# Coarser routing groups, rows stored from ScalarE's queue, a shared ring of banks, and two jobs moved from VectorE to ScalarE

## The chip, the cores and the metric

The kernel runs on one core of one Trainium2 chip. The metric is the device time of one execution in microseconds (us), taken as the median of several runs. The engines are named as in the profile: PE is TensorE, DVE is VectorE, ACT is ScalarE, POOL is GpSimd, SP is SyncE.

## The reference

A gated linear attention over 4 batches, 8 heads, 768 steps and 48 features feeds two mixture-of-experts layers of 3072 tokens, 384 features, 8 experts and 1024 hidden features. In the first layer a token takes part only if its skip score is positive; each token goes to one expert.

```python
# attention, for every step t of a batch and head
state = alpha[:, :, t, :, None] * state + np.einsum('bhd,bhe->bhde', k[:, :, t], v[:, :, t])
y[:, :, t] = np.einsum('bhd,bhde->bhe', q[:, :, t], state)
# first layer (x: tokens by the 384 features of all heads)
do_compute = x @ w_skip > 0
e_idx = np.argmax(xc @ w_gate, axis=1)      # xc: the rows that compute
y[mask] = gate_w[mask, None] * (np.maximum(xc[mask] @ w1[e], 0.0) @ w2[e])   # for each expert e
out[do_compute] = xc + y
# second layer: the same without the skip and without adding x
```

## The kernel before

The attention is cut into 24 chunks of 128 steps (4 batches of 6). The loop over `g` (L744) issues, for each chunk, `emit_a(g + 1)`, `prep(g + 3)`, `emit_y(g)` and `emit_r(g - 1)`, so that four chunks are in work at once. Every engine runs its own instructions in the order in which they are issued.

`prep` runs two scans on DVE (L546 `pp`, L550 `qka`) and two multiplications on POOL (L554, L555). `emit_a` computes the scores `ap` of both halves on PE (L566), masks half 0 on DVE (L574) and half 1 on ACT and POOL (L571, L572), and transposes the keys into `kp` (L581), which ACT copies out (L583); the last chunk of a batch has no `kp`. `emit_y` starts the new state `sp` from the old one (L599; not in the first chunk of a batch), multiplies scores by values into `yp` (L605, L606), adds keys by values to `sp` (L610, L611) and state by queries to `yp` (L614, L615). ACT then copies `yp` out (L618) and DVE multiplies `sp` by the decay, giving the state `s` of the next chunk (L621); the last chunk of a batch has no `sp`. `emit_r` turns the chunk into rows of tokens and router logits at once (`rp`, L642); ACT copies the rows (L643) into a tile `xr` and DVE adds up the logits (L644).

PSUM tiles come from `bank(tag, ...)`: tag B is a ring of four banks (`ap` 0, `ap` 1, `sp`, `yp`), tag K is a single bank, shared by `kp` and `rp`. A tile's first writer waits for the last reader of the tile that held the bank before it.

`route(i)` picks the expert of the tokens of group `i` and works out their places in the experts' lists. It is a generator of small DVE steps; `rt()` runs some of them at points between the attention's instructions (about ten a chunk), so they lie in DVE's queue between the scans. There are 8 groups of 3 chunks (`GROUPS`); `SPLIT` is the number of groups whose tokens (18 chunks) expert list 0 takes. When a group is done, SP's queue stores its rows to `xrows` in DRAM (L679): 384 features, then gate, token number and 8 logits, `ROW` = 394 numbers each. POOL gathers the rows of an expert from there (L441). Small operands (`spot`, `kept`) lie in one PSUM bank of their own.

After chunk 23 the two layers follow, 9 blocks each; their instructions are not touched, except that they take their small operands from the same `spot` places and the same `index`. At `g == 0` two constant matrices are converted (`upper`, `ones`, L757 and L758) and small constants are copied (L761).

Of the kernel before, what the change touches and what calls it, by code (L numbers as in the profile page):

```python
# [8 lines left out]
F32 = mybir.dt.float32  # L9
# [3 lines left out]
AF = mybir.ActivationFunctionType  # L13
ALU = mybir.AluOpType
AX = mybir.AxisListType
# [5 lines left out]
C = 128  # L21
# [22 lines left out]
FIRST = 65536.0  # L44
SX = 64.0
GSCALE = 1.0 / SX
GROUPS = [3] * 8
SPLIT = 6
NWARM = 13

RT = [1, 1, 1, 1, 1, 1, 1, 1, 1, 1, 1, 1, 1, 1, 1, 1, 0, 2, 0, 2, 10, 10, 7, 14]
# [57 lines left out]
def body(tc, qka, vN, rw, wg2, wg17, w1a, w2a, w1b, w2b, cst, zr, out):  # L109
# [3 lines left out]
    with ctx:  # L113
# [6 lines left out]
        def cc(name):  # L120
            o, w = CST[name]
            return cs[:, o:o + w]
# [12 lines left out]
        with ExitStack() as fctx, tc.manual_schedule():  # L135
# [124 lines left out]

            def softmax_pick(l, n, w, res, scale=1.0):

                mx = spot("mx", 6, n, w)
                V.tensor_reduce(mx, l, axis=AX.X, op=ALU.max)
                yield 0
                sh = sm.tile([128, n, w, 8], F32, tag=f"sh{w}", name="sh")
                V.tensor_tensor(sh, l, mx.rearrange("p a (b o) -> p a b o", o=1).to_broadcast([128, n, w, 8]), op=ALU.subtract)
                ex = sm.tile([128, n, w, 8], F32, tag=f"ex{w}", name="ex")
                A.activation(out=ex, in_=sh, func=AF.Exp, scale=scale)
                yield 0  # L270
                eq = sm.tile([128, n, w, 8], F32, tag=f"eq{w}", name="eq")
                de = kept["desc"].rearrange("p (a e) -> p a e", a=1).to_broadcast([128, n * w, 8])
                V.scalar_tensor_tensor(out=eq.rearrange("p a b e -> p (a b) e"), in0=sh.rearrange("p a b e -> p (a b) e"),
                                       scalar=0.0, in1=de, op0=ALU.is_ge, op1=ALU.mult)
                yield 0
                V.tensor_reduce(mx, eq, axis=AX.X, op=ALU.max)
                yield 0
                V.tensor_tensor(eq, eq, mx.rearrange("p a (b o) -> p a b o", o=1).to_broadcast([128, n, w, 8]), op=ALU.is_equal)
                res += [eq, ex]
                yield 0  # L280

            def gates(ex, n, w, res):
                den = spot("den", 6, n, w)
                V.tensor_reduce(den, ex, axis=AX.X, op=ALU.add)
                yield 0
                V.tensor_scalar(den, den, 1e-9, None, op0=ALU.add)
                yield 0
                gw = sm.tile([128, n, w], F32, tag="gw", name="gw") if w == 2 else den
                V.reciprocal(gw, den)
                res.append(gw)  # L290
                yield 0
# [47 lines left out]
            def index(i, n, nl, ohm, on, rk, cols, region, first, last):  # L339

                ad = sm.tile([128, n, nl], F32, tag=f"ad{nl}", name="ad")
                V.tensor_tensor(ad, rk, ohm, op=ALU.mult)
                held[0] = False
                yield 0
                r = sm.tile([128, n, 1], F32, tag=f"r{nl}", name="r")
                V.tensor_reduce(r[:, :, 0], ad, axis=AX.X, op=ALU.add)
                yield 0
                ge = sm.tile([128, n, 4], F32, tag=f"ge{nl}", name="ge")
                V.tensor_tensor(ge, r.to_broadcast([128, n, 4]), kept["th"].rearrange("p (o e) -> p o e", o=1).to_broadcast([128, n, 4]), op=ALU.is_ge)
                yield 0  # L350

                tl = spot("tl", 3, n, 1)
                V.tensor_reduce(tl[:, :, 0], ge, axis=AX.X, op=ALU.add)
                yield 0
                ti = spot("ti", 24, n, 2, 4)
                V.tensor_tensor(ti, cc("seq")[:, 0:4].rearrange("p (a o e) -> p a o e", a=1, o=1).to_broadcast([128, n, 2, 4]),
                                tl.rearrange("p a (o e) -> p a o e", o=1).to_broadcast([128, n, 2, 4]), op=ALU.is_equal)
                yield 0
                pm = sm.tile([128, n, 1], F32, tag=f"pm{nl}", name="pm")
                V.scalar_tensor_tensor(out=pm, in0=tl, scalar=-128.0, in1=r, op0=ALU.mult, op1=ALU.add)  # L360
                w = 8 * sum(t for _, t in cols)
                mv = sm.tile([128, n, 2, w], F16, tag=f"mv{nl}", name="mv")
                o = 0
                for j0, t in cols:
                    V.tensor_tensor(
                        mv.rearrange("p a h c -> p (a h) c")[:, :, o:o + 8 * t].rearrange("p a (e t) -> p a e t", t=t),
                        on.rearrange("p a h e -> p (a h) e")[:, :, j0:j0 + 8].rearrange("p a (e o) -> p a e o", o=1).to_broadcast([128, 2 * n, 8, t]),
                        ti.rearrange("p a h t -> p (a h) t")[:, :, 0:t].rearrange("p a (o t) -> p a o t", o=1).to_broadcast([128, 2 * n, 8, t]), op=ALU.mult)
                    o += 8 * t
                yield 0  # L370
                hot = sm.tile([128, n, 128], F16, tag=f"hot{nl}", name="hot")
                V.tensor_tensor(hot, kept["iota"].rearrange("p (o c) -> p o c", o=1).to_broadcast([128, n, 128]), pm.to_broadcast([128, n, 128]), op=ALU.is_equal)
                yield 1
                yield from wait("indexed", i)
                done["indexed"] += 1
                for k in range(n):
                    T.matmul(idx_ps[:, region, :, NCOL - w:], lhsT=hot[:, k, :], rhs=mv[:, k], start=(first and k == 0), stop=(last and k == n - 1))
                if last:
                    yield 0
                    yield 0  # L380
# [205 lines left out]
            def emit_y(g):  # L586
# [31 lines left out]
                    A.activation(out=y[:, p0:p0 + n], in_=yp, func=AF.Copy)  # L618
                if step_s:
                    sn = wk.tile([GP, NP, D], F32, tag="s", name="s")  # L620
                    V.tensor_tensor(sn, sp, pt.pop(g)[:, :, C:C + 1].to_broadcast([GP, NP, D]), op=ALU.mult)  # L621
                    st["s", g + 1] = sn
                    rt(2)
                if n < NP:
# [9 lines left out]
            def emit_r(g):  # L634

                i, k, n, _ = gof[g]
                if k == 0:
                    xr[i] = em.tile([128, n, ROW], F32, tag="xr", name="xr", bufs=3)
                y = st.pop(("ys", g))
                rp = bank("B" if g == NB - 1 else "K", "rp", NP, 113)  # L640
                for p in range(NP):
                    T.matmul(rp[:, p, :], lhsT=y[:, p, :], rhs=rws[:, p, :], start=True, stop=True)  # L642
                A.activation(out=xr[i][:, k, 0:DM].rearrange("p (a b) -> p a b", a=NP), in_=rp[:, :, 0:96], func=AF.Copy)  # L643
                V.tensor_reduce(lg[:, g, :], rp[:, :, 96:113].rearrange("p a b -> p b a"), axis=AX.X, op=ALU.add)  # L644
                release()
                rt(3)

            def route(i):
# [2 lines left out]
                x = xr[i]  # L651
                l = lg[:, g0:g0 + n, :]
                res = []
                cm = spot("cm", 6, n, 2, 1)
                V.tensor_scalar(cm[:, :, 0, :], l[:, :, 0:1], 0.0, None, op0=ALU.is_gt)
                V.tensor_scalar(cm[:, :, 1, :], l[:, :, 0:1], 0.0, None, op0=ALU.is_le)
                yield from softmax_pick(l[:, :, 1:17].rearrange("p a (w e) -> p a w e", w=2), n, 2, res)
# [6 lines left out]
                def row_ends():  # L664
                    yield from count(n, ohm, before, cum[:, i + 1, :])
                    if i == SPLIT - 1:
                        V.tensor_copy(cum1, cum[:, SPLIT, :])
                        V.memset(cum1[:, 0:1], 0.0)
                    done["counted"] += 1
                    res = []  # L670
                    yield from gates(ex, n, 2, res)
                    den = res[0]
                    V.tensor_tensor(den, den, cm[:, :, :, 0], op=ALU.mult)
                    yield 0
                    V.tensor_reduce(x[:, :, GATE], den, axis=AX.X, op=ALU.add)
                    V.tensor_copy(x[:, :, TOK], kept["tok"][:, g0:g0 + n])
                    V.tensor_tensor(x[:, :, LOG:], l[:, :, 9:17], kept["one"].rearrange("p (a o) -> p a o", o=1).to_broadcast([128, n, 8]), op=ALU.mult)
                    yield 0
                    SY.dma_start(xrows[1 + g0 * 128:1 + (g0 + n) * 128, :].rearrange("(k p) d -> p k d", p=128), x)  # L679

                side = [start(row_ends())]
                on = numbered(n, 16, ohm, g0) if i == len(GROUPS) - 1 else None
# [61 lines left out]
            for g in range(NB):  # L744
# [9 lines left out]
                        finish(*routes[max(i - 2, 0):max(i - 1, 0)])  # L754
                        routes.append(start(route(i)))
                if g == 0:
                    V.tensor_copy(upper, cc("upper"))  # L757
                    V.tensor_copy(ones, cc("ones"))  # L758
                    for name, w in (("desc", 8), ("tok", NB), ("iota", 128), ("seq", 8)):
                        kept[name] = spot(name, w, w, bufs=1)  # L760
                        V.tensor_copy(kept[name], cc(name))  # L761
                    nb = NB + len(TILES1)
# [463 lines left out]
```

## Time and profile before

| what | value |
| --- | --- |
| time, median of 3 runs | 537.44 us (537.41 to 537.68) |
| time of the profiled execution | 539.43 us |
| its span in the profile | 537.7 us |
| mean granted clock of PE | 0.981 |
| busy shares of the span | PE 92%, DVE 69%, ACT 48%, POOL 49% |

The span runs from the first to the last instruction of the profiled execution; some 1.7 us lie around it. A busy share is an average over the attention (until about 154 us) and the two layers behind it.

### The profile page before, as it was taken

What the parts mean: (1) busy time and instruction counts of PE and PEld (TensorE: products, weight loads), DVE (VectorE), ACT (ScalarE), POOL (GpSimd) and SP (SyncE); (2) the same over time, 40 slices, a digit from 0 to 9 for tenths busy, and PEclk for the clock granted to TensorE, in tenths of its full rate; (3) what the DMA queues carried; (4) which work ended last, traced back from release to release, by engine and by line L of the source; (5) the groups of instructions that cost most, each with busy time, mean ns of one, the idle gap of its engine ahead of it and who ended that gap; (6) DMA issues with size and microseconds to landing.
All of it is one profiled execution on the core that took longest, in us unless ns stands there. A gap on an engine that the chain in (4) does not pass through costs nothing.

```text
span 537.7 us, 12030 instructions
## 1 busy us (share of the span) xinstructions
PE 496.3 (92%) x4704; PEld 381.6 (71%) x4704; DVE 371.5 (69%) x1031; ACT 256.4 (48%) x466; POOL 262.3 (49%) x226
## 2 busy tenths in 40 slices
PE   5889898998988999999879989999999999999993
PEld 3678787877877899989879757465555566666662
DVE  7978999999876868888768846863636364646320
ACT  1324343444433566566556415653546364646420
POOL 2366958668625666876947341416215150402121
PEclk9989999999999999999989999999999999999997
DMA  8756877425246667676874158473444535360010
GB/s 304 258 190 209 314 250 264 159 114 208 82 173 209 198 249 229 218 260 199 301 245 145 41 196 275 149 244 123 165 147 140 176 118 208 103 223 28 16 39 26
DMA packets 41460, 96.74 MB, mean 180 GB/s; under 512 B 3641, under 2 KB 28471, under 8 KB 41398
## 3 DMA queue, kind: packets, MB, share of 16 engines
q1 hardware_dynamic: 36662, 82.40, 45.0%
q0 software_dynamic: 4736, 13.51, 7.3%
q8 instruction: 39, 0.64, 0.5%
q14 instruction: 23, 0.19, 0.1%
HBM read 83.41 MB, written 12.99 MB: 179 GB/s over the span
## 4 chain that ended last, share of the span: by engine, by line
PE 56%; DVE 28%; DMA 5%; issue 5%; POOL 2%; ACT 2%; POOLq 0%; DVEq 0%; ACTq 0%
PE hp L464 8%; PE hp L463 8%; PE hp L465 8%; DVE pp L546 6%; DVE qka L550 5%; PE ypc L487 4%; PE ypc L488 4%; PE ypc L489 4%; DMA raw<-in_w1a 3%; PE yp L489 3%; PE yp L488 3%; PE yp L487 3%; PE tp L450 3%; POOL w0l L207 2%; DVE at L574 1%
## 5 line engine op out<-in xcount | busy, mean ns | idle before, releaser
L978 POOL DMA_INDIRECT out<-o,ixo x31 | 31.3, 1009 | 142.2 <-ACT o L1051 125.2
L469 DVE SCALAR_TENSOR_TENSOR h2l<-hp,h2h 128x352 f16<-128x352 f32 (+8 forms) x66 | 38.6, 585 | 64.0 <-ACT h2h L468 63.2
L465 PE MATMUL hp<-x2h,w0l 128*128 128x352 f16 (+8 forms) x216 | 68.7, 323 | 0.0
L463 PE MATMUL hp<-x2h,w0h 128*128 128x352 f16 (+8 forms) x216 | 68.7, 323 | 0.0
L464 PE MATMUL hp<-x2l,w0h 128*128 128x352 f16 (+8 forms) x216 | 68.7, 323 | 0.0
L207 POOL TENSOR_TENSOR w1l<-raw,w1h 128x768 bf16<-128x768 f32 (+1 forms) x26 | 43.0, 1681 | 28.2 <-ACT w1h L202 13.7
L463 PE MATMUL hp<-xh,w0h 128*128 128x200 f16 (+7 forms) x216 | 54.0, 257 | 2.5 <-DVE hl L469 1.4
L468 ACT ACTIVATE h2h<-hp 128x352 f16<-128x352 f32 (+8 forms) x66 | 33.8, 513 | 46.9 <-PE hp L465 45.2
L202 ACT ACTIVATE w0h<-raw 128x768 f16<-128x768 f32 x64 | 53.4, 836 | 4.6 <-DMA raw<-in_w1a 2.7
L441 POOL DMA_INDIRECT xg<-xrows,ix x41 | 49.1, 1197 | 11.6 <-issue 9.8
L464 PEld LDWEIGHTS <-w0h 128*128 128x128 f16 x432 | 43.0, 100 | 16.3 <-issue 3.0
L464 PE MATMUL hp<-xl,w0h 128*128 128x200 f16 (+7 forms) x216 | 53.9, 257 | 0.5 <-DVE xl L452 0.3
L465 PEld LDWEIGHTS <-w0l 128*128 128x128 bf16 x432 | 43.0, 100 | 15.6 <-issue 0.7
L465 PE MATMUL hp<-xh,w0l 128*128 128x200 f16 (+7 forms) x216 | 53.9, 257 | 0.0
L488 PE MATMUL yp<-hl,w1h 128*128 128x200 f16 (+7 forms) x216 | 53.4, 255 | 0.5 <-DVE hl L469 0.5
L487 PE MATMUL yp<-hh,w1h 128*128 128x200 f16 (+7 forms) x216 | 53.5, 255 | 0.0
L202 ACT ACTIVATE w1h<-raw 128x768 f16<-128x768 f32 x64 | 51.5, 836 | 4.1 <-DMA raw<-in_w2a 3.8
L489 PE MATMUL yp<-hh,w1l 128*128 128x200 f16 (+7 forms) x216 | 53.4, 255 | 0.0
L463 PEld LDWEIGHTS <-w0h 128*128 128x128 f16 x432 | 43.0, 100 | 13.6 <-issue 0.5
L554 POOL TENSOR_TENSOR qka<-qka 128x512 f32<-128x512 f32 (+1 forms) x24 | 27.5, 1147 | 47.1 <-DVE qka L550 35.7
L207 DVE TENSOR_TENSOR w0l<-raw,w0h 128x768 bf16<-128x768 f32 x38 | 39.7, 1044 | 14.4 <-ACT w0h L202 12.2
L207 POOL TENSOR_TENSOR w0l<-raw,w0h 128x768 bf16<-128x768 f32 (+1 forms) x26 | 43.2, 1685 | 5.0 <-ACT w0h L202 3.8
(183 smaller groups left out, 1346.2 us busy)
## 6 DMA issues: line engine op xcount, KB each, us to landing
qka<-in_qka SPq DMA_DIRECT2D x21, 772.0 KB, 6.0
raw<-in_w1a SPq DMA_DIRECT2D x8, 1536.0 KB, 6.6
raw<-in_w2a SPq DMA_DIRECT2D x8, 1536.0 KB, 9.4
raw<-in_w1b SPq DMA_DIRECT2D x8, 1536.0 KB, 7.9
raw<-in_w2b SPq DMA_DIRECT2D x8, 1536.0 KB, 7.0
xrows<-xr SPq DMA_DIRECT2D x8, 591.0 KB, 3.7
v<-in_vN SPq DMA_DIRECT2D x24, 192.0 KB, 5.1
xrows<-x SPq DMA_DIRECT2D x9, 197.0 KB, 4.1
```

Of the source, the lines that this page charges most:

```text
L202: A.activation(out=hi[:, sl], in_=r[:, sl], func=AF.Copy)
L207: eng.tensor_tensor(lo[:, sl], r[:, sl], hi[:, sl], op=ALU.subtract)
L441: P.indirect_dma_start(out=dst, out_offset=None, in_=xrows[0:rows], in_offset=bass.IndirectOffsetOnAxis(ap=ix, axis=0), bounds_check=rows ...
L463: T.matmul(hp[:, i], lhsT=wh[:, k, f], rhs=xh[:, k, 0:n], start=(k == 0), stop=False)
L464: T.matmul(hp[:, i], lhsT=wh[:, k, f], rhs=xl[:, k, 0:n], start=False, stop=False)
L465: T.matmul(hp[:, i], lhsT=wl[:, k, f], rhs=xh[:, k, 0:n], start=False, stop=(k == 2))
L468: A.activation(out=hh[:, f0:f0 + nf, 0:n], in_=hp, func=AF.Relu)
L469: V.scalar_tensor_tensor(out=hl[:, f0:f0 + nf, 0:n], in0=hp, scalar=0.0, in1=hh[:, f0:f0 + nf, 0:n], op0=ALU.max, op1=ALU.subtract)
L487: T.matmul(yp, lhsT=wh[:, f, ds], rhs=hs[0][:, f, c0:c1], start=(f == 0), stop=False)
L488: T.matmul(yp, lhsT=wh[:, f, ds], rhs=hs[1][:, f, c0:c1], start=False, stop=False)
L489: T.matmul(yp, lhsT=wl[:, f, ds], rhs=hs[0][:, f, c0:c1], start=False, stop=(f == 7))
L546: V.tensor_tensor_scan(pf, a, bz, initial=0.0, op0=ALU.mult, op1=ALU.add)
```

## The change

Five edits are made together. The routing runs in groups of 6, 6, 6, 3 and 3 chunks, with `SPLIT` at 3 groups, which is still 18 chunks; the places in the PSUM bank `own` grow with it, `pm` moves there, and `iota` is read from where it was loaded. The 384 features of each chunk's rows are stored as soon as they are copied out, by a DMA on ACT's queue; SP's store keeps the last 10 numbers of each row. `rp` always takes a bank of the ring B, so K holds `kp` alone. The conversions of `upper` and `ones` are made by ACT. The multiplication of the new state by the decay is made by ACT in four instructions, one for each pair of heads, where DVE needed one.

```diff
-GROUPS = [3] * 8
-SPLIT = 6
+GROUPS = [6, 6, 6, 3, 3]
+SPLIT = 3
...
-                mx = spot("mx", 6, n, w)
+                mx = spot("mx", 12, n, w)
...
-                pm = sm.tile([128, n, 1], F32, tag=f"pm{nl}", name="pm")
+                pm = spot("pm", 6, n, 1)
...
-                V.tensor_tensor(hot, kept["iota"].rearrange("p (o c) -> p o c", o=1).to_broadcast([128, n, 128]), pm.to_broadcast([128, n, 128]), op=ALU.is_equal)
+                V.tensor_tensor(hot, cc("iota").rearrange("p (o c) -> p o c", o=1).to_broadcast([128, n, 128]), pm.to_broadcast([128, n, 128]), op=ALU.is_equal)
...
                     sn = wk.tile([GP, NP, D], F32, tag="s", name="s")
-                    V.tensor_tensor(sn, sp, pt.pop(g)[:, :, C:C + 1].to_broadcast([GP, NP, D]), op=ALU.mult)
+                    pp = pt.pop(g)
+                    for p in range(NP):
+                        A.activation(out=sn[:, p, :], in_=sp[:, p, :], func=AF.Copy, scale=pp[:, p, C:C + 1])
...
                 if k == 0:
-                    xr[i] = em.tile([128, n, ROW], F32, tag="xr", name="xr", bufs=3)
+                    xr[i] = em.tile([128, n, ROW - DM], F32, tag="xr", name="xr", bufs=3)
                 y = st.pop(("ys", g))
-                rp = bank("B" if g == NB - 1 else "K", "rp", NP, 113)
+                xy = em.tile([128, DM], F32, tag="xy", name="xy", bufs=4)
+                rp = bank("B", "rp", NP, 113)
...
-                A.activation(out=xr[i][:, k, 0:DM].rearrange("p (a b) -> p a b", a=NP), in_=rp[:, :, 0:96], func=AF.Copy)
+                A.activation(out=xy.rearrange("p (a b) -> p a b", a=NP), in_=rp[:, :, 0:96], func=AF.Copy)
+                A.dma_start(xrows[1 + g * 128:1 + (g + 1) * 128, 0:DM], xy)
...
-                    SY.dma_start(xrows[1 + g0 * 128:1 + (g0 + n) * 128, :].rearrange("(k p) d -> p k d", p=128), x)
+                    SY.dma_start(xrows[1 + g0 * 128:1 + (g0 + n) * 128, DM:].rearrange("(k p) d -> p k d", p=128), x)
...
-                    V.tensor_copy(upper, cc("upper"))
-                    V.tensor_copy(ones, cc("ones"))
-                    for name, w in (("desc", 8), ("tok", NB), ("iota", 128), ("seq", 8)):
+                    A.activation(out=upper, in_=cc("upper"), func=AF.Copy)
+                    A.activation(out=ones, in_=cc("ones"), func=AF.Copy)
+                    for name, w in (("desc", 8), ("tok", NB), ("seq", 8)):
```

## Rows read from the trace of the kernel before

**Rows 1.** Stretches: length, busy us of PE, PEld, DVE, ACT, POOL; clock, DMA share, GB/s.
```profile
26.00:34.00 8.00, 6.13 (x70) 5.30 (x69) 7.29 (x10) 1.51 (x3) 5.28 (x4) 0.79 0.28 98
34.00:148.00 114.00, 106.28 (x1480) 91.72 (x1478) 105.36 (x294) 50.59 (x94) 81.35 (x69) 1.00 0.59 206
```

**Rows 2.** PE's waits from 34 to 148 us: total us, times, longest.
```profile
PE kp L581 <- DVE lg L644: 5.2, 7, 1.3
PE rk L312 <- DVE ohm L660: 1.2, 2, 0.7
```

**Rows 3.** Time line of PE from 21 to 36 us: start, length, instruction.
```profile
21.67 0.56 PE L599 MATMUL sp<-s,cs 128*128 128x192 f32 x2 [1.24 <-DVE s L621]
24.64 1.15 PE L642 MATMUL rp<-rws,y 112*128 112x113 f32 x8
25.72 1.49 PE L566 MATMUL ap<-qka 64*128 64x128 f32 x16
29.07 1.04 PE L581 MATMUL kp<-cs,qka 128*128 128x128 f32 x4 [1.87 <-DVE lg L644]
29.91 0.85 PE L599 MATMUL sp<-s,cs 128*128 128x192 f32 x2
34.08 1.15 PE L642 MATMUL rp<-rws,y 112*128 112x113 f32 x8
```

**Rows 4.** Time line of PE in a chunk without a wait.
```profile
67.21 1.15 PE L642 MATMUL rp<-rws,y 112*128 112x113 f32 x8
68.29 1.16 PE L566 MATMUL ap<-qka 64*128 64x128 f32 x16
72.91 1.11 PE L642 MATMUL rp<-rws,y 112*128 112x113 f32 x8
```

**Rows 5.** DVE by line until 156 us: count, busy us, mean ns.
```profile
L621 DVE TENSOR_TENSOR s<-sp,pp 128x192 f32<-128x192 f32 x20 | 6.8, 338 | 0.2
L372 DVE TENSOR_TENSOR hot<-own,pm 128x384 f16<-128x384 f32 x7 | 3.8, 547 | 0.0
L267 DVE TENSOR_TENSOR sh<-lg,own 128x48 f32<-128x48 f32 x7 | 1.3, 191 | 0.0
L758 DVE CAST ones<-cs 128x128 f16<-128x128 f32 x1 | 1.2, 1216 | 0.0
```

**Rows 6.** Time line of PE around 60 us.
```profile
57.81 0.49 PE L599 MATMUL sp<-s,cs 128*128 128x192 f32 x2
60.71 1.15 PE L642 MATMUL rp<-rws,y 112*128 112x113 f32 x8
```

**Rows 7.** Time line of ACT at four places.
```profile
60.88 0.60 ACT L618 ACTIVATE y<-yp 112x512 f32<-112x512 f32 x1 [1.03 <-PE yp L615]
...
95.12 0.59 ACT L583 ACTIVATE ks<-kp 128x512 f32<-128x512 f32 x1
...
396.32 0.52 ACT L468 ACTIVATE h2h<-hp 128x424 f16<-128x424 f32 x1 [1.08 <-PE hp L465]
396.74 0.57 ACT L1051 ACTIVATE o<-tpc,gs 128x384 f32<-128x384 f32 x1
...
449.07 0.21 ACT L451 ACTIVATE x2h<-tp 128x48 f16<-128x48 f32 x1 [1.35 <-PE tp L450]
```

**Rows 8.** ACT by line and shape, whole span.
```profile
L643 ACT ACTIVATE xr<-rp 128x384 f32<-128x384 f32 x24 | 11.8, 491 | 12.8 <-PE rp L642 12.8
L1051 ACT ACTIVATE o<-tpc,gs 128x384 f32<-128x384 f32 x15 | 8.6, 575 | 0.0
```

**Rows 9.** Time line of PE behind the copy of `ks`.
```profile
95.76 1.15 PE L642 MATMUL rp<-rws,y 112*128 112x113 f32 x8 [0.19 <-ACT ks L583]
```

**Rows 10.** Time lines of SP's queue and of POOL behind the last group.
```profile
160.44 0.38 SPq L679 DMA_DIRECT2D xrows<-xr  x1
...
166.13 1.02 POOL L441 DMA_INDIRECT xg<-xrows,ixb  x1 [8.80 <-DVE own L700]
```

**Rows 11.** DMA issues: count, KB, us from issue to landing.
```profile
wg2s<-in_wg SPq DMA_DIRECT2D x1, 12.0 KB, 6.1
```

More of the change, by code (lines that the diff above doesn't have):

```diff
@@ L282, in gates @@
             def gates(ex, n, w, res):
-                den = spot("den", 6, n, w)
+                den = spot("den", 12, n, w)
                 V.tensor_reduce(den, ex, axis=AX.X, op=ALU.add)
@@ L350, in index @@
                 yield 0
-                tl = spot("tl", 3, n, 1)
+                tl = spot("tl", 6, n, 1)
                 V.tensor_reduce(tl[:, :, 0], ge, axis=AX.X, op=ALU.add)
                 yield 0
-                ti = spot("ti", 24, n, 2, 4)
+                ti = spot("ti", 48, n, 2, 4)
                 V.tensor_tensor(ti, cc("seq")[:, 0:4].rearrange("p (a o e) -> p a o e", a=1, o=1).to_broadcast([128, n, 2, 4]),
@@ L653, in route @@
                 res = []
-                cm = spot("cm", 6, n, 2, 1)
+                cm = spot("cm", 12, n, 2, 1)
                 V.tensor_scalar(cm[:, :, 0, :], l[:, :, 0:1], 0.0, None, op0=ALU.is_gt)
@@ L674, in row_ends @@
                     yield 0
-                    V.tensor_reduce(x[:, :, GATE], den, axis=AX.X, op=ALU.add)
-                    V.tensor_copy(x[:, :, TOK], kept["tok"][:, g0:g0 + n])
-                    V.tensor_tensor(x[:, :, LOG:], l[:, :, 9:17], kept["one"].rearrange("p (a o) -> p a o", o=1).to_broadcast([128, n, 8]), op=ALU.mult)
+                    V.tensor_reduce(x[:, :, GATE - DM], den, axis=AX.X, op=ALU.add)
+                    V.tensor_copy(x[:, :, TOK - DM], kept["tok"][:, g0:g0 + n])
+                    V.tensor_tensor(x[:, :, LOG - DM:], l[:, :, 9:17], kept["one"].rearrange("p (a o) -> p a o", o=1).to_broadcast([128, n, 8]), op=ALU.mult)
                     yield 0
-                    SY.dma_start(xrows[1 + g0 * 128:1 + (g0 + n) * 128, :].rearrange("(k p) d -> p k d", p=128), x)
+                    SY.dma_start(xrows[1 + g0 * 128:1 + (g0 + n) * 128, DM:].rearrange("(k p) d -> p k d", p=128), x)
                 side = [start(row_ends())]
```

## The prediction

> **What bounds the kernel now.** The page's busy shares were read first: PE 92%, DVE 69%, ACT 48%. They hide that the attention, where all five edits lie, has limits of its own, so the stretches came next. From 34 to 148 us DVE is busy 105.4 of 114 us and PE 106.3 [rows 1]: both are nearly full, and the reader is to see that work taken off DVE can give back only what PE now loses to waits. PE's waits say how much: 5.2 us in seven waits of `kp` for DVE's sum `lg` (L644), because `kp` and `rp` share one bank and the sum lies in DVE's queue behind two scans, and 1.2 us in two waits of the routing's `rk` [rows 2]. A chunk without a wait takes 72.91 - 67.21 = 5.70 us on PE [rows 4]; this is the floor, and the change takes no matrix work away. The start of the attention is worse. From the first `rp` to the second 34.08 - 24.64 = 9.44 us pass [rows 3], 3.74 more than the floor; 1.87 of it is a wait of `kp` for `lg`, and behind that idle time PE's granted clock falls to a mean of 0.79 from 26 to 34 us [rows 1], so that the stretch from `sp` to `rp` takes 34.08 - 29.91 = 4.17 us [rows 3] instead of 2.90 [rows 6]. A wait of 1.24 us for the state `s` comes before [rows 3]. The cause is DVE, which makes the conversions and small copies there before it masks chunk 2 and scans for chunk 4.
>
> **Part by part: what DVE loses.** A routing group has 27 DVE instructions: `hot` at 0.547 us and 26 others near the 0.191 of `sh` [rows 5], together about 5.5 us. The slope between these two is (547 - 191) / (384 - 48) = 1.06 ns a number. With six chunks `hot` grows by 384 numbers and the rest by about 990, so a large group costs about 5.5 + 1.45 = 7.0 us; three large groups (21 us) take the place of six small ones (33 us). The decay takes 20 x 0.338 = 6.8 us away, the two conversions 2 x 1.2 = 2.4 [rows 5], the copy of `iota` some 0.2. DVE loses about 21 us, but PE's waits are all that this can return.
>
> **What PE gets back.** Between 34 and 148 us: `kp` no longer shares a bank with `rp`, so it waits only for its own `ks` of a chunk earlier; 5.2 us go. What is late next is `yp`, which now takes the bank of the `rp` before; it comes after `kp` and `sp`, about a microsecond later than `kp`, and DVE has less in front of the sum, so I take nothing there. Of the 1.2 us of `rk` half stays with half as many groups in that stretch. That is 5.2 + 0.6 = 5.8 us [rows 2]. At the start: 3.74 + 1.24 = 5.0 us [rows 3, 4]. There `rp` of chunk 0 takes the bank of `ap` 0 of chunk 2, and waits for DVE to mask it behind the small copies that stay: about 0.2 us back. If PE's clock falls all the same, 4.17 - 2.90 = 1.3 us [rows 3, 6] of this are not won.
>
> **What the ring and ACT cost.** In the ring of four the order is now `ap` 0, `ap` 1, `sp`, `yp`, `rp`: five tiles a chunk, so each tile takes the bank of the one after its namesake. `ap` 1 of the next chunk takes the bank of `sp`, which ACT frees only when its four decay instructions are done, and they stand behind its copy of `yp`. Before, it took the bank of `ap` 1, long free. I count from the start of `rp`. ACT's copy of `yp` starts 0.17 later (60.88 against 60.71) and takes 0.60 [rows 6, 7]; the next ACT instruction starts 0.10 before the end of one (396.74 against 396.32 + 0.52 [rows 7]), at 0.67. A copy of 128x48 takes 0.21 [rows 7]; a scale per partition adds 575 - 491 = 84 ns [rows 8], so one decay takes 0.294 and the next follows 0.194 later. The fourth ends at 0.67 + 3 x 0.194 + 0.294 = 1.55, and PE starts 0.05 after an ACT instruction that it waited for (95.76 against 95.12 + 0.59 [rows 7, 9]): 1.60. PE wants `ap` at 1.08 and its half 1 one sixteenth of 1.16 later [rows 4], at 1.15. So PE waits 0.45 us where it did not before. This holds for the chunks 1 to 4 of each batch (in chunk 0 `yp` is ready earlier, chunk 5 has no state), without the very last, after which no `ap` comes: 15 x 0.45 = 6.75 us. Bounds: with no price for the scale and full overlap the fourth ends at 0.67 + 3 x 0.11 + 0.21 = 1.21, the wait is 0.11 and the term 1.7; with no overlap it ends at 0.77 + 4 x 0.294 = 1.95, the wait is 0.85 and the term 12.8. I take 0.45, since both its prices are measured on neighbouring instructions of this engine.
>
> The Trainium skill, "ScalarE: Activation LUTs", section "What ACT_TABLE_LOAD costs", prices an instruction with a per-partition operand at 186 + 93 + 0.833 ns a number, with 93 ns of overlap: 319 ns each and a wait of 0.57, an estimate from that page by which the sum below would end at -1.7 instead of -3.5 us. The rows that stand for the same instruction, 84 ns and 0.10, are shorter together, and no row has this shape with a scale.
>
> Behind the decay ACT copies `rp` and issues the store, 24 times. An issue takes 0.38 on SP's queue [rows 10], and behind it stand the copy of `ap` 1 and of `ks`. Both are used a chunk later, and ACT is busy only 50.6 of 114 us [rows 1], so I cost it at nothing there. In the last two chunks the cover is gone: the copy of the first rows for expert 0 stands behind one store, +0.4 us. SP's store becomes runs of 40 bytes. The nearest row is `wg2s`, 384 runs of 32 bytes, which took 6.1 us to land [rows 11]; the last group's store, issued at 160.44, would then land at 166.5, 0.4 after the first gather wants it at 166.13 [rows 10]. That gather's rows are not the next thing PE needs, so I take 0, and 0.4 is the bound. Everything behind the attention moves with it.
>
> **The sum.** -5.0 + 0.2 - 5.8 + 6.75 + 0.4 = -3.45 us on the profiled execution's own 539.43: 536.0. The median of the runs is 537.44, 2.0 lower; the prediction on it is 534.0 us.
>
> **The rivals.** First, the new wait costs next to nothing (0.11 a chunk): -5.0 + 0.2 - 5.8 + 1.7 + 0.4 = -8.5, 528.9 us. For it: ACT overlaps its short instructions. Against it: each of the four carries a scale. Second, DVE stays late. A large group's 7.0 us fall into about three chunks, 2.3 a chunk against 1.8 before, in which DVE has more to do than now; then `yp` waits for `lg` as `kp` did, about half of the 5.8 us stays, and with the new wait the sum is -0.5: 536.9. Against it: the decay, 0.338 a chunk, has left DVE, and the other half of the chunks has no routing at all. Third, on the other side: the chain of decay on ACT holds `ap` longer than DVE's single instruction ever held PE. It decides from (5.0 - 0.2 + 5.8 - 0.4) / 15 = 0.68 us a chunk; with no overlap (0.85) the sum is +2.6, 540.0 us. For it: the chain is on PE's path in 15 of 24 chunks and each instruction has a fixed cost four times over. The Trainium skill says the same as a rule, "ScalarE: Activation LUTs", section "Rules for kernel authors": a multiplication belongs on VectorE.
>
> **Chances.** The forecast (a wait of 0.25 to 0.6, 531 to 536.3 us) 0.46, the first rival 0.21, the second 0.14, the third 0.19. A change under 0.2%, 1.1 us, can't be told from none in these runs: faster 0.67, same 0.14, slower 0.19. The range runs between the two outer cases, 528.9 to 540.0.
>
> **What would show it.** In the profile after, `kp` waits for no `lg`; DVE is clearly below PE between 34 and 148 us; `ap` (L566) has a wait for ACT `s` of about 0.45 us in chunks 1 to 4; the second `rp` stands near 29.5 us and PE's clock is 1.0 before it. I am wrong if `ap` waits not at all or for 0.7 us and more, if `yp` waits for `lg`, or if the second `rp` still comes after 32 us.

## The result, and the profile after

The changed kernel takes 530.48 us (median of 4 runs, 529.54 to 531.18) against 537.56 us for the kernel before beside it. The ratio is 0.9847 (95% interval 0.9828 to 0.9866), about 8.2 us faster; these two medians alone differ by 7.1 us. The forecast was 534.0 us: the sign was right and the size less than half of what was measured. Of the four cases the first rival (528.9 us), in which the new wait costs next to nothing, is the nearest. One execution of run e7 below (721.87 us, mean granted clock 0.65) and one of e12 (987.26 us, 0.52) count in no median and no ratio.

The profiled execution takes 529.54 us with a span of 527.7 us, 9.9 and 10.0 us less than that of the kernel before. Busy shares, from the page:

```profile
PE 491.6 (93%) x4701; PEld 378.5 (72%) x4701; DVE 363.2 (69%) x927; ACT 270.2 (51%) x545; POOL 274.7 (52%) x226
```

They hardly differ from those of before. The stretches that answer to [rows 1], same columns:

```profile
26.00:34.00 8.00, 7.84 (x121) 6.80 (x122) 6.10 (x9) 3.55 (x10) 7.51 (x6) 1.00 0.69 226
34.00:148.00 114.00, 108.77 (x1500) 94.20 (x1495) 102.56 (x225) 62.77 (x163) 92.83 (x71) 1.00 0.62 205
```

In the first, PE is busy 7.84 of 8 us at a clock of 1.00, where it was 6.13 at 0.79. In the second (which now ends behind the attention), DVE is 6 us less busy than PE; before it was 1 us less. POOL has gone from 81.35 to 92.83 us. PE's waits from 34 to 148 us, answering to [rows 2]:

```profile
PE ap L566 <- POOL qka L555: 2.2, 3, 1.1
PE yp L606 <- POOL at L572: 1.6, 1, 1.6
PE hp L463 <- DVE lg L648: 0.9, 1, 0.9
PE yp L605 <- DVE lg L648: 0.6, 2, 0.3
```

Neither `kp` for `lg` nor `rk` is left, and no row has `ap` waiting for ACT's `s`. PE's time line at the start, answering to [rows 3]:

```profile
23.27 1.15 PE L645 MATMUL rp<-rws,y 112*128 112x113 f32 x8
24.34 1.16 PE L566 MATMUL ap<-qka 64*128 64x128 f32 x16
25.43 0.66 PE L581 MATMUL kp<-cs,qka 128*128 128x128 f32 x4
25.93 0.49 PE L599 MATMUL sp<-s,cs 128*128 128x192 f32 x2
26.58 0.32 PE L605 MATMUL yp<-at,v 128*64 128x128 f32 x1 [0.16 <-DVE lg L648]
```

`ap` takes its undisturbed 1.16 us, here and in each of the 20 chunks behind it, and the second `rp` starts at 29.05 instead of 34.08. ACT beside it:

```profile
23.38 0.60 ACT L618 ACTIVATE y<-yp 112x512 f32<-112x512 f32 x1 [2.16 <-PE yp L615]
23.88 0.87 ACT L623 ACTIVATE s<-sp,pp 128x48 f32<-128x48 f32 x4
24.61 0.52 ACT L646 ACTIVATE xy<-rp 128x384 f32<-128x384 f32 x1
25.16 0.37 ACTq L647 DMA_DIRECT2D xrows<-xy  x1
```

The four instructions of the decay end at 23.88 + 0.87 = 24.75, which is 1.48 us after `rp` began; PE would have wanted that bank at 1.15. So the chain is nearly as long as the prediction priced it (1.55), and yet nobody waits for it.

### The profile page after: what moved, and what is told of

It is laid out like the page before. It is cut to its first block, busy times and chain, and to the rows that moved or that the text cites. A ratio compares the mean times of both kernels' runs of the same rounds, so it can differ in the third digit from the quotient of the medians.

```text
span 527.7 us, 12035 instructions
## 1 busy us (share of the span) xinstructions
PE 491.6 (93%) x4701; PEld 378.5 (72%) x4701; DVE 363.2 (69%) x927; ACT 270.2 (51%) x545; POOL 274.7 (52%) x226
## 4 chain that ended last, share of the span: by engine, by line
PE 59%; DVE 23%; issue 6%; POOL 5%; DMA 4%; ACT 1%; POOLq 0%; ACTq 0%; DVEq 0%
PE hp L463 8%; PE hp L465 8%; PE hp L464 8%; PE ypc L487 4%; PE ypc L489 4%; PE ypc L488 4%; DVE pp L546 4%; DVE qka L550 4%; PE tp L450 3%; PE yp L488 2%; PE yp L489 2%; PE yp L487 2%; DMA xg<-xrows,ixb 2%; PE rp L645 2%; DMA raw<-in_w1a 2%
## 5 line engine op out<-in xcount | busy, mean ns | idle before, releaser
L463 PE MATMUL hp<-xh,w0h 128*128 128x200 f16 (+7 forms) x216 | 52.4, 252 | 4.8 <-DVE hl L469 3.9
L464 PEld LDWEIGHTS <-w0h 128*128 128x128 f16 x432 | 42.3, 98 | 18.5 <-issue 5.2
L464 PE MATMUL hp<-xl,w0h 128*128 128x200 f16 (+7 forms) x216 | 52.3, 252 | 0.1
L465 PE MATMUL hp<-xh,w0l 128*128 128x200 f16 (+7 forms) x216 | 52.4, 252 | 0.0
L463 PEld LDWEIGHTS <-w0h 128*128 128x128 f16 x432 | 42.3, 98 | 13.6 <-issue 0.5
L554 POOL TENSOR_TENSOR qka<-qka 128x512 f32<-128x512 f32 (+1 forms) x24 | 28.5, 1186 | 29.8 <-DVE qka L550 22.9
```

Source lines behind the costliest of these rows:

```text
L463: T.matmul(hp[:, i], lhsT=wh[:, k, f], rhs=xh[:, k, 0:n], start=(k == 0), stop=False)
L464: T.matmul(hp[:, i], lhsT=wh[:, k, f], rhs=xl[:, k, 0:n], start=False, stop=False)
L465: T.matmul(hp[:, i], lhsT=wl[:, k, f], rhs=xh[:, k, 0:n], start=False, stop=(k == 2))
```

## The experiments

Every ratio is to the kernel before, run on the same chip, with its 95% interval; one of these intervals is 0.001 to 0.004 to each side, so differences under some 2 us between two kernels are not told apart. In the expectations, theory A is the prediction's account without its new wait, and theory C says that the amount of DVE's work sets the time.

| kernel | groups of six | rows from ACT | ring | decay on ACT | conversions on ACT | ratio |
| --- | --- | --- | --- | --- | --- | --- |
| e9 | | | | | x | 0.9958 (0.9943 to 0.9972) |
| e10 | | | | x | | 0.9924 (0.9909 to 0.9940) |
| e7 | | | x | | | 1.0049 (1.0024 to 1.0074) |
| e12 | | | x | x | | 0.9902 (0.9876 to 0.9928) |
| e11 | x | x | | | | 0.9977 (0.9959 to 0.9994) |
| e2 | x | x | | x | x | 0.9895 (0.9861 to 0.9929) |
| e3 | x | x | x | | x | 0.9907 (0.9878 to 0.9935) |
| e4 | | x | x | x | x | 0.9933 (0.9908 to 0.9958) |
| e5 | x | x | x | x | | 0.9844 (0.9808 to 0.9879) |
| the change | x | x | x | x | x | 0.9847 (0.9828 to 0.9866) |

**Which bank half 1 of the scores takes.** Run e1 is the changed kernel with the four banks of the ring handed out strictly in turn, as the prediction had assumed.

```diff
                 pool, bufs = phase.get(tag, (ps, 1))
+                if bufs == 4:
+                    tag, bufs = f"B{turns[0] % 4}", 1
+                    turns[0] += 1
...
+            turns = [0]
```

> The changed kernel with the four banks of the ring handed out strictly in turn, so that half 1 of the scores takes the bank of the state before it, as the prediction assumed. Theory A (only the assumed order of the banks was wrong, the length of the wait was right): PE waits for the state's last decay instruction in 15 chunks, 0.3 to 0.45 us each, 5 to 7 us slower than the changed kernel, 535.5 to 537.5 us. Rival B (the wait would have been hidden in any case, behind POOL or DVE): within 1 us of the changed kernel, 529.5 to 531.5 us.

Measured: 535.37 us, ratio 0.9938 (0.9910 to 0.9966), 4.9 us slower than the change by the ratios, close to theory A's 5 to 7 and far from rival B's 1, and 3.5 by the spans (531.2 against 527.7). PE's time line in a chunk without another wait, in e1:

```profile
62.31 1.15 PE L650 MATMUL rp<-rws,y 112*128 112x113 f32 x8
63.39 1.62 PE L571 MATMUL ap<-qka 64*128 64x128 f32 x16
64.93 0.66 PE L586 MATMUL kp<-cs,qka 128*128 128x128 f32 x4
```

and the same chunk of the changed kernel:

```profile
60.83 1.15 PE L645 MATMUL rp<-rws,y 112*128 112x113 f32 x8
61.91 1.16 PE L566 MATMUL ap<-qka 64*128 64x128 f32 x16
63.00 0.66 PE L581 MATMUL kp<-cs,qka 128*128 128x128 f32 x4
```

`ap` lasts 1.62 us instead of 1.16, and `kp` comes 2.62 instead of 2.17 us after `rp`: the wait of 0.45 us, as priced, in the kernel that has it. Behind the first `rp` `ap` takes 1.55 us or more in 12 chunks of e1 and 1.17 to 1.38 in five; in all it is 6.0 us longer than in the change, where 6.75 were forecast. The spans differ by less; PE's waits for POOL are 2.0 us in e1 where the change has 3.8. The wait of `ap` lies inside the row of `ap`, whose 16 matmuls are one group, and the list of PE's waits does not show it. That of the weight loads (PEld) has it, from 34 to 148 us in e1; the change has no such row:

```profile
PEld ap L571 <- ACT s L628: 1.6, 10, 0.2
```

The banks in the programs say why the change lacks it (tile and bank in program order, from the `sp` of one chunk to the `rp` of the next but one):

```
the change  sp:6 yp:5 rp:4  ap0:3 ap1:5 kp:7 sp:6 yp:4 rp:3  ap0:5 ap1:4 kp:7 sp:6 yp:3 rp:5
e1          sp:4 yp:5 rp:7  ap0:3 ap1:4 kp:6 sp:5 yp:7 rp:3  ap0:4 ap1:5 kp:6 sp:7 yp:3 rp:4
e7          sp:6 yp:5 rp:4  ap0:3 ap1:5 kp:7 sp:6 yp:4 rp:3  ap0:5 ap1:6 kp:7 sp:4 yp:3 rp:5
```

The pool does not hand banks out in turn; by what rule it does is not shown here. In the change `ap` 1 takes the bank of `yp` in 18 of the 21 chunks behind the first `rp` (in the other three that of an `ap`); `yp` is read out 0.6 us after ACT's copy begins (23.38 + 0.60 = 23.98), before PE comes for it (24.34). In e1 it takes the bank of `sp` in 18 of them, and then ACT's four instructions are in its way.

**The ring and the decay, each alone and together.** Run e7 is the kernel before with the ring alone.

```diff
-                rp = bank("B" if g == NB - 1 else "K", "rp", NP, 113)
+                rp = bank("B", "rp", NP, 113)
```

> The kernel before with one edit alone, rp in the ring. Theory A (the shared bank passes DVE's lateness on to PE): the 7.1 us of kp's waits go, but DVE is as full as before and yp waits for the same sum a microsecond later, so 1 to 4 us faster than before, 533.5 to 536.5 us. Rival C (DVE's amount of work sets the time): within 1 us of before.

Measured: 541.18 us, ratio 1.0049, 2.6 us slower than before, where theory A had a gain and theory C no difference. PE's waits from 34 to 148 us, and one of them in its time line:

```profile
PE ap L566 <- DVE s L621: 5.8, 6, 1.6
```

```profile
60.35 0.48 PE L566 MATMUL ap<-qka 64*128 64x128 f32 x2
62.43 2.07 PE L566 MATMUL ap<-qka 64*128 64x128 f32 x14 [1.59 <-DVE s L621]
```

The 5.2 us of `kp` are gone as predicted, and 5.8 us of another wait stand in their place. With the decay on DVE the pool gives `ap` 1 the bank of `sp` in 14 chunks (the third line of the list above), so PE waits for DVE's decay, which stands behind two scans, and after this wait of 1.59 us 14 matmuls of `ap` take 2.07 us, where 16 take 1.16 in the change: the mean granted clock from 62 to 66 us is 0.53. So it is no matter of DVE's amount of work, as theory C has it, but of which bank waits for what.

Run e10 is the kernel before with the decay alone.

```diff
-                    V.tensor_tensor(sn, sp, pt.pop(g)[:, :, C:C + 1].to_broadcast([GP, NP, D]), op=ALU.mult)
+                    pp = pt.pop(g)
+                    for p in range(NP):
+                        A.activation(out=sn[:, p, :], in_=sp[:, p, :], func=AF.Copy, scale=pp[:, p, C:C + 1])
```

> The kernel before, with only the decay made by ACT. Theory G: with the decay out of DVE's queue the conversions, still on DVE, start at about 21.1, before POOL's multiplication has begun at 21.4, and last 0.2 us each instead of 1.2; so the mask of chunk 2 again starts 2 us or more earlier. With 0.338 us a chunk off DVE the waits of kp for lg fall from 7.1 to 3 or 4 us. Ratio 0.989 to 0.994 (3 to 6 us). Rival C: DVE's queue is as full without the decay, since its scans stretch against POOL; only the start is won, ratio 0.995 to 0.998. Rival: the parts pay only together with the ring, ratio above 0.998.

Measured: 535.31 us, ratio 0.9924. The wait of `kp` stays, 4.9 us against 5.2, so the expected fall of that wait did not come, though the ratio is the one that theory G gave. Most of the gain lies at the start, where the second `rp` comes at 30.43 instead of 34.08 (some 1.6 us of that is the clock's, as shown below); from there to the last `rp` it is 118.2 us instead of 119.1. The wait that stays:

```profile
PE kp L581 <- DVE lg L646: 4.9, 6, 1.4
```

Run e12 has both: the two diffs of e7 and e10 together.

> The kernel before, with two parts of the change: rp in the ring of banks and the decay on ACT. Theory P (a pair): in the ring without the other part, PE waits for DVE's decay (5.8 us from 34 to 148 us in the run with the ring alone), because half 1 of the scores then takes the bank of the state in most chunks; with the decay on ACT alone, kp still waits for lg (6.5 us). Here half 1 takes the bank of yp, as in the changed kernel, so both waits are gone: below 1 us of PE's waits for s and lg between 34 and 148 us, and a gain clearly over the 4.1 us of the decay alone, 5.5 to 7 us, ratio 0.987 to 0.990. Rival R (the small groups of the routing decide): with both waits gone, PE is held by the routing's rk and idx_ps instead, as in the run with groups of three (6.9 us there), and nothing is won over the decay alone: ratio 0.991 to 0.994.

Measured: 533.56 us, ratio 0.9902. PE's waits, same stretch:

```profile
PE idx_ps L377 <- DVE hot L372: 3.8, 3, 1.5
PE rk L312 <- DVE ohm L662: 1.6, 2, 1.1
```

The waits for `lg` and for `s` are both gone, as theory P says; but the routing's own results, 5.4 us, are what PE waits for now, as rival R says. Behind two of these waits, each of 1.5 us, PE's clock falls besides (a mean of 0.79 from 84 to 92 us and 0.83 from 118 to 128), while in the change it is 1.00 from 34 to 148 us. The ratio lies between the two and is not told apart from that of the decay alone. Only the groups of six take these away.

The same square at the other end, in the changed kernel. Run e2 puts `rp` back on the bank K (the diff of e7, reversed):

> The changed kernel with rp back in the single bank K. Theory A (the shared bank held PE, by the sum that lies late in DVE's queue): kp waits for that sum again; DVE has less to do, so less than the 7.1 us of before, but 2 to 5 us come back, 532.5 to 535.5 us. Rival C (the relief of DVE alone made the gain, the bank was only where it showed): no wait over 0.5 us in all, 530 to 531.5 us.

Measured: 532.32 us, ratio 0.9895, 2.6 us slower than the change, as theory A says. From 34 to 148 us `kp` waits again:

```profile
PE kp L581 <- DVE lg L648: 3.0, 3, 1.5
```

Run e3 puts the decay back on DVE (the diff of e10, reversed):

> The changed kernel with the decay of the state back on DVE, one instruction a chunk. Theory A (DVE is no longer what holds PE once the bank is its own): 20 times 0.34 us more on DVE are mostly hidden, 0 to 2 us slower, 530.5 to 532.5 us. Rival C (DVE's amount of work sets the time): 20 times 0.26 to 0.34 us come back, 5 to 7 us, 535.5 to 537.5 us.

Measured: 533.13 us, ratio 0.9907, 3.2 us slower than the change; theory A had 0 to 2, theory C 5 to 7, and neither holds. What is there is the wait of e7, for `ap` 1 takes the bank of `sp` in 11 chunks:

```profile
PE ap L566 <- DVE s L621: 2.3, 4, 1.2
```

Besides, PE waits 1.2 us before `sp` at the start again, and the first `rp` comes at 24.67 instead of 23.27.

**The start and the conversions.** Run e5 is the changed kernel with the conversions back on DVE.

```diff
-                    A.activation(out=upper, in_=cc("upper"), func=AF.Copy)
-                    A.activation(out=ones, in_=cc("ones"), func=AF.Copy)
+                    V.tensor_copy(upper, cc("upper"))
+                    V.tensor_copy(ones, cc("ones"))
```

> The changed kernel with the two conversions back on DVE. Theory A (the start gained because DVE no longer makes PE wait and let its clock fall before chunk 4): the second rp comes 2 to 4 us later than in the changed kernel (29.1 us there), the clock may fall, 2.5 to 5 us slower, 532.5 to 535.5 us. Rival E (the bank of its own alone repaired the start): 0 to 1 us slower, 529.5 to 531.5 us.

Measured: 530.14 us, ratio 0.9844, no difference, as rival E says; the second `rp` starts at 28.91. The prediction had taken 2 x 1.2 us off DVE with them. The time line of DVE and POOL in the kernel before shows what these 1.2 us were:

```profile
21.19 0.33 DVE L621 TENSOR_TENSOR s<-sp,pp 128x192 f32<-128x192 f32 x1
21.36 1.18 POOL L554 TENSOR_TENSOR qka<-qka 128x512 f32<-128x512 f32 x1 [3.60 <-DVE qka L550]
21.44 1.18 DVE L757 CAST upper<-cs 128x128 f16<-128x128 f32 x1
22.50 1.18 POOL L555 TENSOR_TENSOR qka<-qka,pp 128x512 f32<-128x512 f32 x1
22.54 1.22 DVE L758 CAST ones<-cs 128x128 f16<-128x128 f32 x1
```

Each conversion begins just after a multiplication of POOL and ends 0.08 us after it. The decay, at 21.19, stands ahead of them on DVE. With the decay gone from in front of them (e5) they begin before POOL does:

```profile
21.12 0.20 DVE L761 CAST upper<-cs 128x128 f16<-128x128 f32 x1
21.23 0.22 DVE L762 CAST ones<-cs 128x128 f16<-128x128 f32 x1
```

0.42 us, not 2.4. The Trainium skill, "SBUF — State Buffer", section "Who interferes with whom", says that a cast on VectorE in its fast mode and a GpSimd instruction lock one shared pair of ports for the whole instruction, and that the one issued second is blocked fully. The trace agrees: 1.18 and 1.22 us behind POOL, 0.20 and 0.22 ahead of it.

Run e9 is the other half: the kernel before with the conversions alone on ACT (the diff above, reversed).

> The kernel before, with only the two conversions made by ACT. Theory G: in the kernel before each conversion lasts 1.2 us on DVE, and ends within 0.1 us of a multiplication that POOL had begun just before it (21.36 + 1.18 and 22.50 + 1.18); it only waits for POOL, and that time stands on DVE's queue ahead of the mask of chunk 2. On ACT it is gone: the mask starts about 2.2 us earlier (near 23.1 instead of 25.31), the second rp 2 to 3 us earlier than 34.08, and the time falls by 1.5 to 2.5 us, ratio 0.995 to 0.997. Rival E (from the run with the conversions back on DVE): they are worth nothing, ratio 0.999 to 1.001, and whatever was lost on them is made up before 60 us.

Measured: 536.88 us, ratio 0.9958, 2.3 us: theory G. The mask of chunk 2 starts at 23.11 and the second `rp` comes at 30.73. In e10 too, with the conversions on DVE and the decay away, they last 0.20 and 0.22 us, the mask starts at 23.07 and the second `rp` comes at 30.43. So either edit takes away the same two waits of DVE for POOL, and with the decay gone the conversions have nothing more to win there (e5).

**The groups.** Run e4 is the changed kernel with the 8 groups of three.

```diff
-GROUPS = [6, 6, 6, 3, 3]
-SPLIT = 3
+GROUPS = [3] * 8
+SPLIT = 6
```

> The changed kernel with eight routing groups of three chunks. Theory A: 12 us of DVE work come back in 100 us in which DVE had about 10 us to spare, so DVE holds PE again in part: 2 to 5 us slower, 532.5 to 535.5 us. Rival C (DVE's amount of work sets the time): the whole of about 10 us comes back, 538 to 541 us. Rival D (routing is hidden by the ring's slack): within 1 us.

Measured: 534.9 us, ratio 0.9933, within what A gives. From 34 to 148 us PE waits for the routing:

```profile
PE idx_ps L377 <- DVE hot L372: 3.9, 3, 1.7
PE rk L312 <- DVE ohm L664: 3.0, 5, 1.5
```

Run e11 is the kernel before with the groups of six and the rows from ACT's queue, and none of the other three edits (e2 with the decay and the conversions on DVE).

> The kernel before, with the groups of six and the rows stored from ACT's queue, but with rp on the shared bank, the decay and the conversions on DVE. If the parts simply add, this is the rest of the gain: the decay is worth 3.3 us and the ring 2.6 when taken out of the changed kernel, of 8.2, so this one would give 2 to 3 us, ratio 0.994 to 0.996. If they give back the same waits (the waits of PE for DVE's late sum), each is worth more alone than when taken last: 4 to 6 us here, ratio 0.989 to 0.993. Rival: the large groups come late with their rows and there is no gain without the ring, ratio above 0.998.

Measured: 537.86 us, ratio 0.9977, 1.2 us: less than either account gave, and the rival's "above 0.998" lies inside the interval. The wait of `kp` for `lg` is 3.9 us there. Alone the groups, with the rows' queue, are worth 1.2 us; taken out of the change the groups are worth 4.6 (0.9933 - 0.9847): they pay once the ring and the decay have taken the other waits away.

**The rows' queue.** Run e6 is the changed kernel with the 24 stores issued from SP's queue.

```diff
-                A.dma_start(xrows[1 + g * 128:1 + (g + 1) * 128, 0:DM], xy)
+                SY.dma_start(xrows[1 + g * 128:1 + (g + 1) * 128, 0:DM], xy)
```

> The changed kernel with each chunk's rows stored from SP's queue instead of ACT's. Theory A (the issue costs ACT nothing on PE's path, except about 0.4 us at the end): 0 to 0.5 us faster or the same, 529.5 to 531 us. Rival F (on SP's queue the stores stand in front of the loads of v and qka and hold them): DVE or POOL wait for loads, 1 to 4 us slower.

Measured: 534.23 us, ratio 0.9929, 4.4 us slower than the change by the ratios and 2.6 by the spans: rival F. SP's queue in e6 and, below, in the change:

```profile
25.17 0.35 SPq L647 DMA_DIRECT2D xrows<-xy  x1
25.62 0.38 SPq L537 DMA_DIRECT2D v<-in_vN  x1
26.10 0.40 SPq L531 DMA_DIRECT2D qka<-in_qka  x1
```

```profile
22.38 0.33 SPq L537 DMA_DIRECT2D v<-in_vN  x1
23.42 0.33 SPq L531 DMA_DIRECT2D qka<-in_qka  x1
```

The store waits for ACT's copy `xy` (87.2 us over 21 waits in SP's queue), and the loads for the chunk three ahead stand behind it: `qka` is issued 2.7 us later. DVE's first scan then waits for it:

```profile
DVE pp L546 <- DMA qka<-in_qka: 5.3, 4, 2.4
```

against 2.4 us in 1 wait in the change. So the queue of the store is a part of the change that the prediction costed only on ACT's side.

**POOL.** The waits that are new in the change are for POOL, so run e8 gives DVE the four subtractions of expert weights that POOL makes during the attention.

```diff
-ON_POOL = [(0, 2)] + [(1, 2, 3)] * 8 + [()] * 7
+ON_POOL = [()] + [(1, 2, 3)] * 8 + [()] * 7
```

> The changed kernel with the two parts of each weight tile of the first expert that POOL subtracted during the attention (four in all) given to DVE. Theory G (POOL is what PE now waits for: its multiplications and masks are stretched and late by 3.8 us in all): the waits for POOL shrink, 1 to 3 us faster than the changed kernel, 527.5 to 529.5 us. Rival H (DVE and POOL hold each other, and what POOL loses DVE gets): within 1 us, or slower.

Measured: 531.58 us, ratio 0.9885 (0.9851 to 0.9919), 2 us slower than the change at about the limit of the intervals. POOL's busy time from 34 to 148 us falls from 92.83 to 78.52 us and DVE's rises from 102.56 to 104.71; the waits for POOL fall only from 3.8 to 2.6 us, 1.1 us of `rk` come in and those of `yp` for `lg` grow from 0.6 to 1.4 us, as rival H says. No run beat the changed kernel by more than the intervals tell.

## Why the prediction was right in sign and wrong in size

**The step that failed** is "`ap` 1 of the next chunk takes the bank of `sp`", and with it the term 15 x 0.45 = 6.75 us. The premise was that five tiles over four banks make each tile take the bank of the one after its namesake. The pool does not do this; in the changed kernel `ap` 1 takes the bank of `yp` in 18 of 21 chunks, and the wait is nil in the trace. Nor did the kernel before hand its banks out in turn: there `ap` 1 took the bank of an `ap` 0 in 9 of these 21 chunks, not always that of an `ap` 1. Run e1 builds what was assumed and has the wait at 0.45 us; its ratio would put the kernel at 0.9938 x 537.44 = 534.1 us, where the forecast was 534.0. That they agree so closely is luck in part: against the forecast both the wait (4.9 us by the ratios instead of 6.75) and the gain without it (8.2 instead of 10.2) came out smaller. The price of the chain on ACT was nearly right, 1.48 us from `rp` to its end (the lines of ACT above) against 1.55, and 307 ns for one instruction (x80) against 294:

```profile
L623 ACT ACTIVATE s<-sp,pp 128x48 f32<-128x48 f32 x80 | 17.3, 307 | 0.0
```

The Trainium skill, "ScalarE: Activation LUTs", section "What ACT_TABLE_LOAD costs", gives 319 ns by estimate; the measured 307 lies between it and the forecast's 294. The bounds on that wait, 1.7 to 12.8 us, held no place for none of it, because both ends were prices of the same premise.

**The sum without this term** is -10.2 us on the profiled execution; the spans differ by 10.0 and the ratio says 8.2. Its parts:

- The start, -5.0 + 0.2: the second `rp` went from 34.08 to 29.05, -5.0; the first came 1.4 us earlier and the second 5.78 behind it instead of 9.44. The size holds, the reasons only in part. `rp` of chunk 0 took the bank of `ap` 1 of chunk 2, not of `ap` 0, and the 0.2 does not show: no wait of `rp` is listed before 34 us. The conversions cost DVE so much only through POOL (e5, e9, e10), and the fall of PE's clock, priced at 1.3 us, need not come with the wait: e11 has the same wait of 1.87 us of `kp` for `lg` and no fall, and from that `kp` to the next `rp` it takes 3.39 us where the kernel before took 34.08 - 29.07 = 5.01. So 1.6 us of the 5.0 are the clock's. That this explains also why the spans differ by more than the ratio says is likely and not shown. Time lines and stretches of e11, and last the stretch of the kernel before:

```profile
24.67 1.15 PE L643 MATMUL rp<-rws,y 112*128 112x113 f32 x8
28.78 0.66 PE L581 MATMUL kp<-cs,qka 128*128 128x128 f32 x4 [1.87 <-DVE lg L646]
32.17 1.15 PE L643 MATMUL rp<-rws,y 112*128 112x113 f32 x8
```

```profile
30.00:34.00 4.00, 4.00 (x68) 3.65 (x64) 3.09 (x5) 1.16 (x3) 4.00 (x3) 1.00 0.35 81
30.00:34.00 4.00, 4.00 (x51) 3.40 (x50) 3.36 (x4) 0.60 (x1) 4.00 (x3) 0.67 0.02 4
```

- The middle, -5.8: from the second to the last `rp` it is (153.21 - 34.08) - (144.16 - 29.05) = 4.0 us. Both waits of [rows 2] are gone altogether, more than forecast. What is late next was not `yp` alone (0.6 us) but POOL, 3.8 us in four waits, which the prediction did not look at.
- The end, +0.4: nothing. From the last `rp` to the first `hp` pass 1.96 us in both kernels. Behind that point the layers take 381.6 instead of 382.5 us; over the other traces of this study it is 380.6 to 383.1, so this 0.9 is not the change's.

**The rivals.** The first one came nearest to the time, with 528.9, by a price of 0.11 us a chunk; the measured price is none, for another reason than ACT's overlap. The second, DVE late, hardly occurred: `yp` waits 0.6 us for `lg`, where it had half of 5.8. The third, the chain on ACT, did not occur either. The Trainium skill, "ScalarE: Activation LUTs", section "Rules for kernel authors", puts a multiplication on VectorE; here the measurement decides against it, for with the decay on DVE (e3) the kernel is 3.2 us slower.

**What the prediction left out** is that the parts do not add. Apart, the decay is worth 4.1 us, the groups with the rows' queue 1.2 and the ring minus 2.6, together 2.7, or 5.0 with the 2.3 of the conversions, which win the same start as the decay; the change has 8.2. The ring takes away the wait for `lg`, but hands `ap` 1 a bank that DVE frees late; with the decay on ACT the pool gives it another bank; both together leave PE waiting for the routing, and the groups remove that.

## What to carry to other kernels

When a tile joins a shared ring of banks, read from the built program which bank each tile really takes, and price the wait for that bank's last reader, before pricing the reader's chain. Follow each edit to the wait that comes next, for edits that look separate (a ring, an instruction on another engine, larger groups) can each move one wait into the next and pay only together. A long duration in a row may be a wait for another engine: compare its start and end with that engine's instructions before costing it as work that can be moved.

## What the runs showed of the hardware

DVE's scans and POOL's two-input multiplications stretch each other where they meet. In the changed kernel, DVE and POOL around 70 us:

```profile
69.58 1.18 POOL L554 TENSOR_TENSOR qka<-qka 128x512 f32<-128x512 f32 x1 [2.83 <-DVE qka L550]
70.72 2.12 POOL L555 TENSOR_TENSOR qka<-qka,pp 128x512 f32<-128x512 f32 x1
```

```profile
66.78 1.23 DVE L546 TENSOR_TENSOR_SCAN pp<-qka,bz 128x520 f32<-128x520 f32 x1
70.13 1.73 DVE L546 TENSOR_TENSOR_SCAN pp<-qka,bz 128x520 f32<-128x520 f32 x1
72.11 1.83 DVE L550 TENSOR_TENSOR_SCAN qka<-qka,bz 128x520 f32<-128x520 f32 x1
```

A scan alone takes 1.23 us. The one at 70.13 begins while L554 runs and takes 0.50 longer; L555, begun at 70.72 while that scan runs, takes 2.12 instead of 1.18; the scan at 72.11 begins inside L555 and takes 1.83. From 34 to 148 us L555 has a mean of 1223 ns before and 1729 after.

```profile
L555 POOL TENSOR_TENSOR qka<-qka,pp 128x512 f32<-128x512 f32 x19 | 23.2, 1223 | 0.0
```

```profile
L555 POOL TENSOR_TENSOR qka<-qka,pp 128x512 f32<-128x512 f32 x18 | 31.1, 1729 | 0.0
```

This is most of what POOL's busy time gained, and part of what DVE lost in small instructions it got back in longer scans (L550 from 1369 to 1510 ns). In the runs with groups of three (e4, e7, e9, e10 and e12) L555 is at 1219 to 1271, in those with groups of six at 1431 to 1730, so it comes with the large groups; by what path is not shown.

A wait of PE can come with a fall of its clock, and need not. Behind its wait of 1.87 us the kernel before has a mean granted clock of 0.67 from 30 to 34 us, with 0.50 (the lower of the two levels, 1.2 GHz) from 30 to 32; behind the same wait e11 keeps 1.00. In e7 and e12 waits of 1.5 to 1.6 us came with such a fall as well. So a term of a sum that rests on one fall of the clock is not one that each run pays.
